# Rank counts as one column instead of 128, one comparison for five one-hots, and stores ahead of loads in an attention and expert kernel

## The chip, the cores and the metric

The program runs on 1 core of one Trainium2 chip. Its metric is the time of one execution on the device in microseconds (us): the median of 3 runs of the kernel before is 224.98 us (224.42 to 225.13). TensorE is called PE here, VectorE DVE, ScalarE ACT, GpSimd POOL, SyncE SP. SP only issues DMAs in this program; PEld is the part of PE that loads weights.

## What is computed

For 8 batches of 576 tokens, attention runs over 8 heads of width 64 in chunks of 64 tokens. Its output x (576 x 512 per batch) goes through a gated expert: each batch picks its 128 tokens with the highest gate score, those rows go through two matrix products, and the result is added back to them.

```python
scores = scale * np.matmul(q_c, k_c.transpose(0, 1, 2, 4, 3))       # per chunk of 64
attn = np.exp(scores - max); attn = attn / (np.sum(attn, axis=-1, keepdims=True) + 1e-09)
out = np.matmul(attn, v_c)                                          # -> x[b, token, 512]
scores = np.einsum('bsd,d->bs', x, w_gate)
for b in range(B):
    top_idx = np.argpartition(-scores[b], capacity)[:capacity]      # 128 of 576
    ye = np.maximum(x[b, top_idx] @ w1, 0.0) @ w2                   # 512 -> 1024 -> 512
    g = 1.0 / (1.0 + np.exp(-scores[b, top_idx]))
    out[b, top_idx] = x[b, top_idx] + g[:, None] * ye
```

## The kernel before, in words

**Units and steps.** The 4608 tokens are cut into 36 units of 128. A main loop runs one step after another (line 537). In step t it makes the scores of unit t, the transposes of unit t-1 and the values of unit t-2, so each unit passes through three steps: s (scores in PSUM), m and d (maximum and difference, DVE), t (transposes in PSUM), e (exponential, ACT), o (values in PSUM), den, rc and x (the normalised output, DVE). The tile x is stored to `out` and multiplied by the gate vector (prod, on POOL, summed by ACT; for units 8, 17, 26 and 35 by one DVE instruction), which gives one column of scores, sc.

**Ranking.** Nine units hold two batches: an even one of 4.5 units and an odd one. For each batch the scores are laid along a row by PE transposes (to_row), and DVE compares each of five blocks of tokens with the tokens before it and in it: cmp is the table of 0 and 1, and the same instruction counts its ones into a column of acc. The rank of a token is its count in acc plus what the later blocks have over it; that second part is the column sum of later blocks' cmp, so it is a PE product with cmp as the weights. rank_sums (line 305) makes it, and it makes it 128 columns wide, with a ramp 0..127 in a first product (ones against ramp), so that in every column k stands k minus the sum. rank_hot (line 322) compares that with acc and gives a one-hot table hot (token against rank); the last block, over which nothing stands, gets its own instruction from io and acc. rank_idx multiplies hot by token numbers and score parts (rt): idx are the 128 tokens, sg their scores. POOL then gathers those rows from `out` (xe), PE transposes them (expert_in), and two batches together make one round of expert products.

**The expert products.** ffn is a list of matmuls that the loop takes from in portions (quotas): so many after the scores, so many after place a, and so many after place b of a step. Each weight is split into a high part (ACT copies it into w1h, w2h) and a rest (POOL subtracts: w1l, w2l); a product is three matmuls. From the start of the first round on (step 13), PE always has such work to fill with.

**What sets the order.** Every engine takes its instructions in the order in which the program text issues them (class InOrder, line 62). Three tables set where the rarer parts stand: PLANS (lines 50 to 54) gives step and place of each ranking part for the first pair of batches (FIRST) and for the three other pairs (OTHER, 9 steps further for each pair), DOTS the units summed by DVE, WPLAN (line 58) for each of eight weight pieces the step of its load, and the places of its high part and its rest. The places of a step are, in order: pre, s0, s1, s2, a, b, c, d.

**Memory.** Inputs of a unit (qkvt, 772 KB) rotate through 5 buffers: the load of unit t+2 is issued in step t and waits for the values of unit t-3. Weights pass through 4 staging buffers (wst). One PSUM bank r serves all ranking parts and the transposes of xe, so each of these waits until the one before it has been read. SP issues loads, stores and weight loads in one queue; in a step the load stands ahead of the store, and the weight load behind both (lines 540 to 543).

Of the kernel before, what the change touches and what calls it, by code (L numbers as in the profile page):

```python
# [9 lines left out]
BF16 = mybir.dt.bfloat16  # L10
F16 = mybir.dt.float16
I32 = mybir.dt.int32
AF = mybir.ActivationFunctionType
ALU = mybir.AluOpType
# [6 lines left out]
CH = 64  # L21
CAP = 128
P = 128

NU = B * S // P
# [8 lines left out]
NTC = 5  # L34
# [14 lines left out]

FIRST = dict(rowe=(7, "a"), row4=(7, "b"), esum=(8, "s0"), ehot=(8, "s2"), eidx=(8, "b"), rowo=(10, "a"), row8=(10, "a"),  # L50
             osum=(11, "s0"), ohot=(11, "s2"), oidx=(11, "s2"), exin=(11, "a"), oxin=(12, "d"), ffn=(12, "d"))
OTHER = dict(rowe=(8, "b"), row4=(9, "b"), esum=(10, "a"), ehot=(10, "a"), eidx=(10, "c"), rowo=(11, "a"), row8=(11, "c"),
             osum=(12, "b"), ohot=(12, "b"), oidx=(13, "a"), exin=(13, "c"), oxin=(14, "c"), ffn=(14, "c"))
PLANS = (FIRST, OTHER, OTHER, OTHER)

DOTS = (8, 17, 26, 35)

WPLAN = ((9, (10, "c"), (11, "s0")), (10, (11, "c"), (11, "d")), (11, (12, "b"), (12, "d")), (12, (13, "b"), (13, "d")),
         (13, (14, "b"), (15, "d")), (14, (15, "b"), (16, "d")), (15, (16, "b"), (17, "d")), (16, (17, "b"), (18, "d")))


class InOrder:
# [22 lines left out]
def attention_moe(ctx: ExitStack, tc: tile.TileContext, qkv, wrep, w1, w2, consts, outs):  # L85
    nc = tc.nc
    pe, dve, act, pool, sp = (InOrder(tc, e) for e in (nc.tensor, nc.vector, nc.scalar, nc.gpsimd, nc.sync))

    cp = ctx.enter_context(tc.tile_pool(name="cp", bufs=1))
# [8 lines left out]
    con = cp.tile([P, C_N], F32, name="con")  # L98
    wr = cp.tile([P, DM], F32, name="wr")
    ltm = cp.tile([P, 5 * P], BF16, name="ltm")  # L100
    io = cp.tile([P, CAP], F16, name="io0")
    ones = cp.tile([33, P], BF16, name="ones")
    ramps = [cp.tile([33, 4, CAP], BF16, name=f"ramp{s}") for s in range(2)]
    accs = [cp.tile([P, NTC + 1], F32, name=f"acc{i}") for i in range(4)]
    one = cp.tile([P, CAP], BF16, name="one")
    ident = con[:, C_ID:C_ID + P]

    w1h = [cp.tile([P, NKT, 2 * P], F32R, name=f"w1h{k}") for k in range(NFT // 2)]
# [6 lines left out]
    def load(u, parts=None):  # L115
        t = iop.tile([P, UW], F32, name="qkvt")
        for e, lo, hi in parts or ((sp, 0, UW),):
            e.dma_start(out=t[:, lo:hi], in_=qkv[u][:, lo:hi])
        loaded[u] = t
# [23 lines left out]
    def scores(u):  # L143
# [4 lines left out]
        for h in range(HP):  # L148
            for r in range(2):
                R = slice(r * D, (r + 1) * D)  # L150
                for c in range(2):
                    pe.matmul(s[c * CH:(c + 1) * CH, r, h * CH:(h + 1) * CH], q[R, h, c, :], k[R, h, c, :],
                              start=True, stop=True)
# [16 lines left out]
    def r_bank(g, held=False):  # L170
        if g == 0 and not held:
            return ps_f.tile([P, 512], F32, name="f", tag="f")
        return ps_r.tile([P, 512], F32, name="r")
# [16 lines left out]
    def values(u):  # L190
        e = st_e.pop(u)
        v = loaded.pop(u)[:, 2 * QW:UW].rearrange("p (c h e) -> p c h e", c=2, h=HP)
        o = ps_v.tile([P, 2, 512], F32, name="o")
        for h in range(HP):
            for j in range(2):
                R = slice(j * CH, (j + 1) * CH)
                for c in range(2):
                    C = slice(c * CH, (c + 1) * CH)
                    pe.matmul(o[C, j, h * VW:(h + 1) * VW], e[R, h, C], v[R, c, h, :], start=True, stop=True)
        o4 = o[:, :, 0:HP * VW].rearrange("p j (h e) -> p j h e", e=VW)  # L200
        den = wk.tile([P, 2, HP], F32, name="den")
        act.activation(out=den, in_=o4[:, :, :, D], func=AF.Copy, bias=1e-9)
        st_o[u] = o4, den
# [45 lines left out]
    whole = slice(0, P)  # L249

    def blocks(s):


        if s == 0:
            return [(c, whole, c * P) for c in range(4)] + [(4, halves[0], 4 * P)]
        return [(4, halves[1], S)] + [(c, whole, c * P) for c in range(5, UPG)]
# [8 lines left out]
    def rank_cmp(b, i, row, part="all"):  # L265
# [4 lines left out]
        s = b % 2  # L270
        col, R, t0 = blocks(s)[i]
        n = R.stop - R.start
        before = t0 - s * S
# [30 lines left out]

    def rank_sums(b):


        r = rk[b]
        s = b % 2
        bl = blocks(s)  # L310
        cs = r_bank(b // 2, held=b == 0).rearrange("p (c k) -> p c k", c=4)
        for i in range(NTC - 1):
            Ri = bl[i][1]
            o = bl[i][2] - s * S
            n = Ri.stop - Ri.start
            pe.matmul(cs[Ri, i, :], ones[:, 0:n], ramps[s][:, i, :], start=True, stop=False)
            for j in range(i + 1, NTC):
                Rj = bl[j][1]
                pe.matmul(cs[Ri, i, :], r["cmp"][j][Rj, o:o + n], one[Rj], start=False, stop=(j == NTC - 1))
        r["cs"] = cs  # L320

    def rank_hot(b):
        r = rk[b]
        bl = blocks(b % 2)
        hot = r["hot"] = wk.tile([P, NTC, CAP], BF16, name="hot", bufs=2)
        for R, lo, hi in ((whole, 0, 4),) if b % 2 == 0 else ((bl[0][1], 0, 1), (whole, 1, 4)):
            n = hi - lo
            dve.tensor_tensor(
                out=hot[R, lo:hi, :], in0=r["cs"][R, lo:hi, :],
                in1=r["acc"][R, lo:hi].rearrange("p (c o) -> p c o", o=1).broadcast_to([R.stop - R.start, n, CAP]),  # L330
                op=ALU.is_equal)
        R = bl[4][1]
        dve.tensor_scalar(out=hot[R, 4, :], in0=io[R], scalar1=r["acc"][R, 5:6], scalar2=r["acc"][R, 4:5],
                          op0=ALU.subtract, op1=ALU.is_equal)

    rts = [cp.tile([P, NTC, 6], BF16, name=f"rt{i}") for i in range(4)]

# [123 lines left out]
    nload = 1  # L461
    while nload < NIO:
        load(nload)
        if nload == 2:
            sp.dma_start(out=wr, in_=wrep)
        nload += 1
    dve.memset(one, 1.0)
    dve.memset(ltm[:, 0:4 * P], -TINY)
    di = wk.tile([P, DF], F32, name="wst", bufs=4)
    pool.iota(di[:, 0:P], pattern=[[1, P]], base=0, channel_multiplier=-1, allow_small_or_imprecise_dtypes=True)  # L470
    dve.tensor_scalar(out=ltm[:, 4 * P:], in0=di[:, 0:P], scalar1=0.0, scalar2=-TINY, op0=ALU.is_lt, op1=ALU.mult)
    dj = wk.tile([P, DF], F32, name="wst", bufs=4)
    pool.iota(dj[:, 0:CAP], pattern=[[1, CAP]], base=0, channel_multiplier=0, allow_small_or_imprecise_dtypes=True)
    dve.tensor_copy(io, dj[:, 0:CAP])

    pool.iota(dj[0:1, 4 * CAP:8 * CAP], pattern=[[P, 4], [0, CAP]], base=-(4 * P), channel_multiplier=0,
              allow_small_or_imprecise_dtypes=True)
    dve.memset(ones, 1.0)
    for s, ramp in enumerate(ramps):
        dve.memset(ramp, 0.0)  # L480
        for c in range(4):
            dve.tensor_copy(ramp[32:33, c, :], dj[32:33, 0:CAP])
        dve.tensor_scalar(out=ramp[0:1].rearrange("p c k -> p (c k)"), in0=dj[0:1, 4 * CAP:8 * CAP],
                          scalar1=0.0 if s else float(CH), scalar2=None, op0=ALU.add)
    for i, rt in enumerate(rts):
        dve.tensor_copy(rt[:, :, 0:3], con[:, C_TOK + (i % 2) * 3 * NTC:C_TOK + (i % 2 + 1) * 3 * NTC]
                        .rearrange("p (c k) -> p c k", k=3))
# [5 lines left out]
    def at(when, f, *a, dt=0):  # L493
        events.setdefault((when[0] + dt, when[1]), []).append((f, a))

    fill = []
    for u in range(NU):
        c = u % UPG
# [6 lines left out]
    for g in range(NG):  # L505
        q = PLANS[g]
        t = UPG * g
        e, o = 2 * g, 2 * g + 1
        for f, k, a in (
# [5 lines left out]
            at(q[k], f, *a, dt=t)  # L515
    for i, (t, h, l) in enumerate(WPLAN):
        src, hi, lo = (w1, w1h, w1l) if i < 4 else (w2, w2h, w2l)
        at((t, "pre"), weight_load, src, i % 4)
        for k in range(2):
            at(h, weight_hi, src, i % 4, k, hi)  # L520
            at(l, weight_lo, src, i % 4, k, hi, lo)
# [9 lines left out]
    def run(step, place):  # L531
        for f, a in events.pop((step, place), []):
            f(*a)

    step = 0
    started = False
    while step < NU + 2 or events or fill:
        here = step < NU
        quota = [q for t, q in QUOTAS if t <= step][-1]
        if 2 < step and nload < NU:  # L540
            load(nload)
            nload += 1
        run(step, "pre")
        late = bool(fill)
        if late and 0 <= step - 2 < NU:
            values(step - 2)
        if here:
            scores(step)
        if not late:
            if 0 <= step - 1 < NU:  # L550
                transposes(step - 1)
            run(step, "s0")
            if 0 <= step - 2 < NU:
                values(step - 2)
        run(step, "s1")
        if late and 0 <= step - 2 < NU:
            normalise(step - 2)
        if here:
            maxima(step)
        run(step, "s2")  # L560
        if here:
            differences(step)
        if not late and 0 <= step - 2 < NU:
            normalise(step - 2)
        started = started or bool(fill)
        if not started:
            keep_warm(WARMS[min(step, len(WARMS) - 1)])
        run_fill(quota[0])
        if late and 0 <= step - 1 < NU:
            transposes(step - 1)  # L570
        run(step, "a")
        run_fill(quota[1])
        run(step, "b")
        run_fill(quota[2])
        run(step, "c")
        run(step, "d")
        step += 1


# [36 lines left out]
```

## Time and profile before

| what | value |
|---|---|
| median of 3 runs | 224.98 us (224.42 to 225.13) |
| profiled execution, its own time | 223.23 us |
| span of that profile | 221.5 us |
| mean granted TensorE clock | 0.955 |
| PE busy | 200.1 us (90% of the span), 3303 instructions |
| DVE busy | 134.3 us (61%), 345 instructions |
| POOL busy | 101.1 us (46%) |
| ACT busy | 79.0 us (36%) |
| DMA moved | 47.12 MB, mean 213 GB/s |

All terms are read in one profiled execution, whose own time, 223.23 us, is 1.73 us more than its span. The engines run side by side, so an engine's busy time says little by itself: what counts is, stretch by stretch, which engine or transfer the others wait for. A number in brackets at the end of a row of the timeline is the idle time of that engine in front of the row, and what ended it. Every row carries line 72, that of the helper that issues all instructions, so instructions are told apart by their tiles, written as out<-in.

### The profile page before, as it was taken

The numbers are of one execution on the slowest core, as the hardware profiler recorded it, in microseconds if no ns is written. First come the engines' busy times: TensorE is split into PE (matmuls) and PEld (weight loads), VectorE is DVE, ScalarE is ACT, GpSimd is POOL, SyncE is SP. The second block draws the span as 40 slices with busy tenths as digits, with TensorE's granted clock in tenths as the row PEclk, the third lists the DMA queues.
The fourth block names the chain that finished last, engine by engine and source line by source line (L and its number), as shares of the span: only waits on it lengthen the run. The fifth ranks groups of instructions, "written<-read, shape, count | busy, mean of one in ns | idle before, by whom it ended". The sixth has DMA issues, their size and how long they took to land.

```text
span 221.5 us, 7738 instructions
## 1 busy us (share of the span) xinstructions
PE 200.1 (90%) x3303; PEld 162.2 (73%) x3303; DVE 134.3 (61%) x345; ACT 79.0 (36%) x198; POOL 101.1 (46%) x116
## 2 busy tenths in 40 slices
PE   7787669699699989979999999899999989999990
PEld 2455547476599887667789988578899867899890
DVE  6578668767454377778685986666767644322120
ACT  2135322514448675112454553223455230212100
POOL 2024433356864699954464454508154671110031
PEclk9999996955799999999999999999999999999997
DMA  6999985998999887467899885658431110210011
GB/s 209 405 301 305 382 302 167 326 407 279 319 339 371 289 313 263 137 230 246 268 304 272 257 289 170 230 172 281 143 114 70 60 47 7 90 47 0 3 53 41
DMA packets 13777, 47.12 MB, mean 213 GB/s; under 512 B 1712, under 2 KB 2352, under 8 KB 13744
## 3 DMA queue, kind: packets, MB, share of 16 engines
q1 hardware_dynamic: 12160, 42.18, 55.7%
q0 software_dynamic: 1296, 4.20, 5.5%
q8 instruction: 26, 0.43, 0.8%
q10 hardware_dynamic: 288, 0.26, 0.4%
q14 instruction: 7, 0.06, 0.1%
HBM read 35.09 MB, written 11.53 MB: 211 GB/s over the span
## 4 chain that ended last, share of the span: by engine, by line
PE 49%; DVE 9%; POOL 7%; DMA 4%; ACT 4%; issue 2%; POOLq 1%; DVEq 0%
PE f L72 31%; PE r L72 7%; PE o L72 5%; PE s L72 3%; PE t L72 3%; DVE cmp L72 3%; DMA xe<-out,idx 3%; POOL prod L72 2%; POOL w2l L72 2%; POOL hl L72 2%; ACT prod L72 1%; DVE x L72 1%; DVE d L72 1%; DVE hot L72 1%; POOL w1l L72 1%
## 5 line engine op out<-in xcount | busy, mean ns | idle before, releaser
L72 POOL TENSOR_TENSOR prod<-x,wr 128x512 f32<-128x512 f32 x32 | 40.9, 1281 | 22.3 <-DVE x L72 22.1
L72 ACT ACTIVATE e<-t 128x512 f32<-128x512 f32 x36 | 21.5, 597 | 50.5 <-PE t L72 50.4
L72 PE MATMUL f<-xh,w1h 128*128 128x256 f32 x128 | 38.1, 297 | 0.0
L72 PE MATMUL f<-xl,w1h 128*128 128x256 f32 x128 | 36.8, 288 | 0.2 <-DVE ge L72 0.2
L72 PE MATMUL f<-xh,w1l 128*128 128x256 f32 x128 | 36.6, 286 | 0.0
L72 PE MATMUL o<-qkvt,e 64*64 64x65 f32 x1152 | 27.8, 232 | 4.0 <-issue 4.0
L72 PEld LDWEIGHTS o<-qkvt,e 64*64 64x64 f32 x1152 | 21.9, 141 | 9.8 <-issue 7.2
L72 PE MATMUL s<-qkvt 64*64 64x64 f32 x1152 | 26.4, 234 | 2.6 <-DMA qkvt<-qkv 2.1
L72 DVE TENSOR_TENSOR x<-o,rc 128x512 f32<-128x512 f32 x36 | 24.9, 692 | 6.2 <-DVE rc L72 2.8
L72 PE MATMUL f<-w2h,hh 128*128 128x512 f32 (+1 forms) x72 | 28.1, 391 | 0.0
L72 PEld LDWEIGHTS s<-qkvt 64*64 64x64 f32 x1152 | 22.5, 146 | 7.4 <-issue 2.1
L72 POOL DMA_INDIRECT out<-y,idx x9 | 9.1, 1006 | 39.7 <-DVE y L72 39.4
L72 PE MATMUL f<-w2l,hh 128*128 128x512 f32 (+1 forms) x72 | 27.1, 376 | 0.0
L72 PE MATMUL f<-w2h,hl 128*128 128x512 f32 (+1 forms) x72 | 27.0, 375 | 0.0
L72 DVE TENSOR_REDUCE m<-s 128x8 f32<-128x512 f32 x36 | 24.6, 683 | 3.8 <-PE s L72 3.7
L72 DVE TENSOR_TENSOR d<-s,m 128x512 f32<-128x512 f32 x36 | 24.9, 691 | 1.2
L72 POOL TENSOR_TENSOR hl<-hr,hh 128x512 fp32r<-128x512 f32 x12 | 15.4, 1286 | 20.9 <-ACT hh L72 16.9
L72 PEld LDWEIGHTS f<-xh,w1h 128*128 128x128 f32 x128 | 24.3, 190 | 0.9
L72 PEld LDWEIGHTS f<-xl,w1h 128*128 128x128 f32 x128 | 24.4, 190 | 0.8 <-DVE ge L72 0.4
L72 ACT ACTIVATE prod<-prod 128x512 f32<-128x512 f32 x32 | 20.0, 626 | 12.4 <-POOL prod L72 12.4
L72 PEld LDWEIGHTS f<-xh,w1l 128*128 128x128 f32 x128 | 24.3, 190 | 0.2
L72 PE MATMUL t<-con,d 128*128 128x128 f32 x144 | 23.4, 287 | 0.0
(74 smaller groups left out, 283.3 us busy)
## 6 DMA issues: line engine op xcount, KB each, us to landing
qkvt<-qkv SPq DMA_DIRECT2D x35, 772.0 KB, 5.6
out<-x SPq DMA_DIRECT2D x32, 256.0 KB, 4.9
wst<-w SPq DMA_DIRECT2D x8, 512.0 KB, 6.6
out<-x SPq DMA_DIRECT2D x8, 128.0 KB, 3.9
qkvt<-qkv SPq DMA_DIRECT2D x1, 260.0 KB
qkvt<-qkv ACTq DMA_DIRECT2D x2, 128.0 KB, 3.1
qkvt<-qkv SPq DMA_DIRECT2D x2, 128.0 KB, 2.9
wr<-wrep SPq DMA_DIRECT2D x1, 256.0 KB, 6.8
```

The costliest lines, as they stand in the source:

```text
L72: ins = f(*a, **k).ins
```

## The change

1. **Sums.** rank_sums now makes one column per block instead of 128. Two products with the identity (ident, in con) copy acc's columns into PSUM, one of five columns and one for the second count of the last block; ten products of a cmp block with a column of minus ones follow in the same bank. ones, ramps and one are gone.
2. **One-hots.** rank_hot is one comparison of 640 columns, of a table io5 (two versions, made at the start) with the five sums, each spread over 128 columns. It was two instructions for even batches and three for odd ones. All four acc tiles are set to zero at the start.
3. **Places.** For pairs 2 to 4: the last block's row and comparison (row8) go from place c of step 11 to place a of step 12; the odd sums and one-hots (osum, ohot) from b to c of step 12; the odd index and gather (oidx) from a to b of step 13.
4. **SP.** Place pre, with the store, now runs before the load of the step; in step 11 the load goes to the end of the step.
5. **Weights.** The first w1 piece is loaded in step 11 instead of 9, the second at the end of 11 instead of in 10, the third at the end of 12 instead of in 11. Their high parts go to 12 a, 12 d and 13 b (from 10 c, 11 c, 12 b), their rests to 12 b, 13 s1 and 13 d (from 11 s0, 11 d, 12 d). The five pieces behind them are loaded, copied and split exactly one step later.

```diff
-OTHER = dict(... row8=(11, "c"), osum=(12, "b"), ohot=(12, "b"), oidx=(13, "a"), ...)
+OTHER = dict(... row8=(12, "a"), osum=(12, "c"), ohot=(12, "c"), oidx=(13, "b"), ...)
-WPLAN = ((9, (10, "c"), (11, "s0")), ...
+WPLAN = (((11, "s1"), (12, "a"), (12, "b")), ...
...
-        cs = r_bank(b // 2, held=b == 0).rearrange("p (c k) -> p c k", c=4)
+        cs = r["cs"] = r_bank(b // 2, held=b == 0)[:, 0:NTC]
+        pe.matmul(cs, ident, r["acc"][:, 0:NTC], start=True, stop=False)
+        pe.matmul(cs[:, 4:5], ident, r["acc"][:, 5:6], start=False, stop=False)
...
-            pe.matmul(cs[Ri, i, :], ones[:, 0:n], ramps[s][:, i, :], start=True, stop=False)
             for j in range(i + 1, NTC):
                 Rj = bl[j][1]
-                pe.matmul(cs[Ri, i, :], r["cmp"][j][Rj, o:o + n], one[Rj], start=False, stop=(j == NTC - 1))
+                pe.matmul(cs[Ri, i:i + 1], r["cmp"][j][Rj, o:o + n], minus[Rj], start=False, stop=(i, j) == (NTC - 2, NTC - 1))
...
-        for R, lo, hi in ((whole, 0, 4),) if b % 2 == 0 else ((bl[0][1], 0, 1), (whole, 1, 4)):
-            n = hi - lo
-            dve.tensor_tensor(
-                out=hot[R, lo:hi, :], in0=r["cs"][R, lo:hi, :],
-                in1=r["acc"][R, lo:hi].rearrange("p (c o) -> p c o", o=1).broadcast_to([R.stop - R.start, n, CAP]),
-                op=ALU.is_equal)
-        R = bl[4][1]
-        dve.tensor_scalar(out=hot[R, 4, :], in0=io[R], scalar1=r["acc"][R, 5:6], scalar2=r["acc"][R, 4:5],
-                          op0=ALU.subtract, op1=ALU.is_equal)
+        dve.tensor_tensor(out=hot, in0=io5[b % 2], in1=r["cs"].rearrange("p (c o) -> p c o", o=1).broadcast_to([P, NTC, CAP]),
+                          op=ALU.is_equal)
...
-        at((t, "pre"), weight_load, src, i % 4)
+        at(t, weight_load, src, i % 4)
...
-        if 2 < step and nload < NU:
+        run(step, "pre")
+        if 2 < step and step != 11 and nload < NU:
             load(nload)
             nload += 1
-        run(step, "pre")
...
         run(step, "d")
+        if step == 11:
+            load(nload)
+            nload += 1
         step += 1
```

**Place one: the odd sums of the second pair (step 21), on PE.** Names: sc are score columns, o and s values and scores of two units, t transposes, f expert products, cmp the comparison tables. Before:

```order
L72 MATMUL r<-con,sc 128x128
L72 MATMUL o<-qkvt,e 64x65 x16
L72 MATMUL s<-qkvt 64x64 x16
...
L72 MATMUL t<-con,d 128x128 x4
L72 MATMUL f<-w2h_99,hh_1162 128x512
L72 MATMUL f<-w2l_103,hh_1162 128x512
L72 MATMUL f<-w2h_99,hl_1163 128x512
L72 LDWEIGHTS ones
L72 MATMUL r<-ramp_85,ones 64x128
L72 LDWEIGHTS cmp_1703
L72 MATMUL r<-one,cmp_1703 64x128
```

The same place with the change:

```order
L73 MATMUL o<-qkvt,e 64x65 x16
L73 MATMUL s<-qkvt 64x64 x16
...
L73 MATMUL t<-con,d 128x128 x4
L73 MATMUL r<-con,sc 128x128
L73 MATMUL f<-w2h_97,hh_1140 128x512
...
L73 MATMUL f<-w2h_98,hl_1237 128x512
L73 MATMUL r<-acc_87,con 128x5
L73 MATMUL r<-acc_87,con 128x1
L73 LDWEIGHTS cmp_1684
L73 MATMUL r<-minus,cmp_1684 64x1
```

The last block's transpose (r<-con,sc) has gone from the end of a step to the middle of the next one, and the sums behind three more expert products. Each sum used to have 14 pairs of weights and matmul (4 with ones, 10 with cmp); now it has the two identity products and 10 pairs.

**Place two: the same stretch on DVE.** m and d belong to step 21, y is the end of an expert round. Before:

```order
L72 SCALAR_TENSOR_TENSOR cmp_1709,acc_89<-r,sc,ltm 128x448
L72 SCALAR_TENSOR_TENSOR cmp_1709,acc_89<-r,sc,ltm 128x128
...
L72 TENSOR_TENSOR d<-s,m 128x2x4x64
L72 SCALAR_TENSOR_TENSOR y<-f,g,xe 128x512
L72 TENSOR_TENSOR hot<-r,acc_89 64x128
L72 TENSOR_TENSOR hot<-r,acc_89 128x384
L72 TENSOR_SCALAR hot<-io_82,acc_89 128x128
```

With the change:

```order
L73 SCALAR_TENSOR_TENSOR cmp_1690,acc_87<-r,sc,ltm 128x448
...
L73 TENSOR_TENSOR d<-s,m 128x2x4x64
L73 SCALAR_TENSOR_TENSOR y<-f,g,xe 128x512
L73 SCALAR_TENSOR_TENSOR cmp_1690,acc_87<-r,sc,ltm 128x128
L73 TENSOR_TENSOR hot<-io_83,r 128x640
```

The last comparison stood ahead of the step's rc, x, m and d; it now stands behind them and behind y, right in front of the one-hot.

**Place three: SP, steps 9 to 13.** qkvt is the load of a unit, out its store, wst a weight piece. Before:

```order
L72 DMA qkvt<-qkv 128x1544
L72 DMA out<-x 128x512
L72 DMA wst<-w 128x1024
L72 DMA qkvt<-qkv 128x1544
L72 DMA out<-x 128x512
L72 DMA wst<-w 128x1024
```

With the change, from the store of step 11 on:

```order
L73 DMA out<-x 128x512
L73 DMA wst<-w 128x1024 x2
L73 DMA qkvt<-qkv 128x1544
L73 DMA out<-x 128x512
L73 DMA qkvt<-qkv 128x1544
L73 DMA wst<-w 128x1024
L73 DMA out<-x 128x512
L73 DMA wst<-w 128x1024
L73 DMA qkvt<-qkv 128x1544
```

The three DMAs of a step before went load, store, weight; now the store, which waits for x, stands in front, and the first weight pieces come two steps later in a bunch.

## Rows read from the trace of the kernel before

**Rows 1.** Windows: busy us (instructions) per engine, granted clock, DMA share, GB/s.
```profile
5.00:36.00 31.00, 24.28 (x588) 16.69 (x590) 21.83 (x52) 9.78 (x27) 8.39 (x10) 0.97 0.87 314
36.00:60.00 24.00, 20.32 (x376) 14.43 (x376) 15.63 (x43) 9.81 (x26) 15.10 (x16) 0.71 0.94 324
60.00:90.00 30.00, 28.96 (x551) 25.63 (x544) 18.42 (x43) 18.23 (x43) 22.48 (x22) 0.98 0.91 322
90.00:191.50 101.50, 98.02 (x1622) 81.28 (x1621) 68.38 (x181) 36.64 (x95) 50.08 (x59) 1.00 0.55 179
```

**Rows 2.** Timeline of PE from 90 us: start us, length us, instruction, [idle before <-releaser].
```profile
91.64 0.18 PE L72 MATMUL r<-rt,hot 64*128 64x6 bf16 x1 [0.47 <-DVE hot L72]
...
97.30 0.29 PE L72 MATMUL r<-con,sc 128*128 128x128 f32 x1 [1.21 <-DVE cmp L72]
...
139.65 0.29 PE L72 MATMUL r<-con,sc 128*128 128x128 f32 x1 [0.90 <-DVE cmp L72]
...
179.88 0.29 PE L72 MATMUL r<-con,sc 128*128 128x128 f32 x1 [0.64 <-DVE cmp L72]
```

**Rows 3.** Chain that ended last: start us, us on the chain, what.
```profile
100.71 1.64 PE r L72 x14
...
105.09 0.44 PE t L72 x4
105.53 0.29 PE r L72 x5
...
130.63 1.52 PE r L72 x14
...
133.88 0.20 PE r L72 x5
```

**Rows 4.** Timeline of PE in step 11: first instruction of the sums, first behind them.
```profile
46.40 0.31 PE L72 MATMUL f<-ramp,ones 33*64 33x128 bf16 x1
...
48.84 1.15 PE L72 MATMUL o<-qkvt,e 64*64 64x65 f32 x32
```

**Rows 5.** Tile hot: count, ns min/median/max, first and last start, forms.
```profile
L72 DVE TENSOR_TENSOR hot<-r,acc x10: 295/558/692, 34.2 to 184.0; 128x512 bf16<-128x512 f32 x4, 64x128 bf16<-64x128 f32 x3, 128x384 bf16<-128x384 f32 x3
```

**Rows 6.** Timeline of DVE, steps 19 and 21.
```profile
90.16 0.69 DVE L72 TENSOR_TENSOR hot<-r,acc 128x512 bf16<-128x512 f32 x1
90.77 0.81 DVE L72 TENSOR_SCALAR hot<-io,acc 64x128 bf16<-64x128 f16 x1
...
100.21 0.69 DVE L72 TENSOR_TENSOR d<-s,m 128x512 f32<-128x512 f32 x1
100.81 0.74 DVE L72 SCALAR_TENSOR_TENSOR y<-f,g,xe 128x512 f32<-128x512 f32 x1
```

**Rows 7.** Timeline of POOL, 90 to 151 us.
```profile
90.25 1.28 POOL L72 TENSOR_TENSOR prod<-x,wr 128x512 f32<-128x512 f32 x1
91.49 2.53 POOL L72 TENSOR_TENSOR w2l<-wst,w2h 128x512 fp32r<-128x512 f32 x2
...
106.93 1.00 POOL L72 DMA_INDIRECT xe<-out,idx  x1 [2.73 <-DVE sg L72]
...
150.68 1.01 POOL L72 DMA_INDIRECT out<-y,idx  x1 [0.30 <-issue]
```

**Rows 8.** Timeline of PE: transposes of gathered rows in steps 12 and 23.
```profile
57.58 0.75 PE L72 MATMUL r<-con,xe 128*128 128x128 f32 x4 [1.67 <-DMA xe<-out,idx]
...
110.80 0.63 PE L72 MATMUL r<-con,xe 128*128 128x128 f32 x4
```

**Rows 9.** Tile xe: its gathers from issue to landing.
```profile
DMA to landing us min/median/max: 3.3/4.0/6.7
```

**Rows 10.** Timeline of SP, steps 4 and 5: load of unit 6, store of unit 1.
```profile
15.93 0.33 SPq L72 DMA_DIRECT2D qkvt<-qkv  x1
17.17 0.34 SPq L72 DMA_DIRECT2D out<-x  x1
```

**Rows 11.** Timeline of PE: scores of unit 6.
```profile
22.35 0.69 PE L72 MATMUL s<-qkvt 64*64 64x64 f32 x32 [1.10 <-DMA qkvt<-qkv]
```

More of the change, by code (lines that the diff above doesn't have):

```diff
@@ L51 @@
              osum=(11, "s0"), ohot=(11, "s2"), oidx=(11, "s2"), exin=(11, "a"), oxin=(12, "d"), ffn=(12, "d"))
-OTHER = dict(rowe=(8, "b"), row4=(9, "b"), esum=(10, "a"), ehot=(10, "a"), eidx=(10, "c"), rowo=(11, "a"), row8=(11, "c"),
-             osum=(12, "b"), ohot=(12, "b"), oidx=(13, "a"), exin=(13, "c"), oxin=(14, "c"), ffn=(14, "c"))
+OTHER = dict(rowe=(8, "b"), row4=(9, "b"), esum=(10, "a"), ehot=(10, "a"), eidx=(10, "c"), rowo=(11, "a"), row8=(12, "a"),
+             osum=(12, "c"), ohot=(12, "c"), oidx=(13, "b"), exin=(13, "c"), oxin=(14, "c"), ffn=(14, "c"))
 PLANS = (FIRST, OTHER, OTHER, OTHER)
 DOTS = (8, 17, 26, 35)
-WPLAN = ((9, (10, "c"), (11, "s0")), (10, (11, "c"), (11, "d")), (11, (12, "b"), (12, "d")), (12, (13, "b"), (13, "d")),
-         (13, (14, "b"), (15, "d")), (14, (15, "b"), (16, "d")), (15, (16, "b"), (17, "d")), (16, (17, "b"), (18, "d")))
+WPLAN = (((11, "s1"), (12, "a"), (12, "b")), ((11, "d"), (12, "d"), (13, "s1")), ((12, "d"), (13, "b"), (13, "d")),
+         ((13, "pre"), (14, "b"), (14, "d")), ((14, "pre"), (15, "b"), (16, "d")), ((15, "pre"), (16, "b"), (17, "d")),
+         ((16, "pre"), (17, "b"), (18, "d")), ((17, "pre"), (18, "b"), (19, "d")))
 class InOrder:
@@ L100, in attention_moe @@
     ltm = cp.tile([P, 5 * P], BF16, name="ltm")
-    io = cp.tile([P, CAP], F16, name="io0")
-    ones = cp.tile([33, P], BF16, name="ones")
-    ramps = [cp.tile([33, 4, CAP], BF16, name=f"ramp{s}") for s in range(2)]
+    io5 = [cp.tile([P, NTC, CAP], F16, name=f"io5{s}") for s in range(2)]
     accs = [cp.tile([P, NTC + 1], F32, name=f"acc{i}") for i in range(4)]
-    one = cp.tile([P, CAP], BF16, name="one")
+    minus = cp.tile([P, 1], BF16, name="minus")
     ident = con[:, C_ID:C_ID + P]
@@ L315, in rank_sums @@
             n = Ri.stop - Ri.start
-            pe.matmul(cs[Ri, i, :], ones[:, 0:n], ramps[s][:, i, :], start=True, stop=False)
             for j in range(i + 1, NTC):
                 Rj = bl[j][1]
-                pe.matmul(cs[Ri, i, :], r["cmp"][j][Rj, o:o + n], one[Rj], start=False, stop=(j == NTC - 1))
-        r["cs"] = cs
+                pe.matmul(cs[Ri, i:i + 1], r["cmp"][j][Rj, o:o + n], minus[Rj], start=False, stop=(i, j) == (NTC - 2, NTC - 1))
     def rank_hot(b):
         r = rk[b]
-        bl = blocks(b % 2)
         hot = r["hot"] = wk.tile([P, NTC, CAP], BF16, name="hot", bufs=2)
-        for R, lo, hi in ((whole, 0, 4),) if b % 2 == 0 else ((bl[0][1], 0, 1), (whole, 1, 4)):
-            n = hi - lo
-            dve.tensor_tensor(
-                out=hot[R, lo:hi, :], in0=r["cs"][R, lo:hi, :],
-                in1=r["acc"][R, lo:hi].rearrange("p (c o) -> p c o", o=1).broadcast_to([R.stop - R.start, n, CAP]),
-                op=ALU.is_equal)
-        R = bl[4][1]
-        dve.tensor_scalar(out=hot[R, 4, :], in0=io[R], scalar1=r["acc"][R, 5:6], scalar2=r["acc"][R, 4:5],
-                          op0=ALU.subtract, op1=ALU.is_equal)
+        dve.tensor_tensor(out=hot, in0=io5[b % 2], in1=r["cs"].rearrange("p (c o) -> p c o", o=1).broadcast_to([P, NTC, CAP]),
+                          op=ALU.is_equal)
     rts = [cp.tile([P, NTC, 6], BF16, name=f"rt{i}") for i in range(4)]
@@ L466, in attention_moe @@
         nload += 1
-    dve.memset(one, 1.0)
+    dve.memset(minus, -1.0)
     dve.memset(ltm[:, 0:4 * P], -TINY)
@@ L472, in attention_moe @@
     dj = wk.tile([P, DF], F32, name="wst", bufs=4)
-    pool.iota(dj[:, 0:CAP], pattern=[[1, CAP]], base=0, channel_multiplier=0, allow_small_or_imprecise_dtypes=True)
-    dve.tensor_copy(io, dj[:, 0:CAP])
-    pool.iota(dj[0:1, 4 * CAP:8 * CAP], pattern=[[P, 4], [0, CAP]], base=-(4 * P), channel_multiplier=0,
+    pool.iota(dj[:, 0:NTC * CAP], pattern=[[P, NTC], [1, CAP]], base=-(4 * P), channel_multiplier=0,
               allow_small_or_imprecise_dtypes=True)
[L478 to L484, printed above, removed]
+    for s in range(2):
+        for lo, hi in ((0, 4), (4, 5)):
+            dve.tensor_scalar(out=io5[s][:, lo:hi].rearrange("p c k -> p (c k)"), in0=dj[:, lo * CAP:hi * CAP],
+                              scalar1=float(CH) if s == 0 and lo == 0 else 0.0, scalar2=None, op0=ALU.add)
+    for acc in accs:
+        dve.memset(acc, 0.0)
     for i, rt in enumerate(rts):
```

## The prediction

> **What bounds the kernel now.** I read the windows first. They cut the span into four regimes [rows 1]. From 5 to 36 us the DMA engines are the busiest thing (share 0.87) and PE is busy 24.28 of 31.00 us. From 36 to 60 us the granted clock averages 0.71, so PE spends much of it at the lower of its two levels (1.2 of 2.4 GHz), and the DMA share is 0.94. From 60 to 90 us PE is busy 28.96 of 30.00 us with the DMA still at 0.91 and POOL at 22.48. From 90 us to 191.5 us PE is busy 98.02 of 101.50 us at full clock and the DMA has room (0.55). So after 90 us every microsecond taken from PE's list, and every one in which PE stands, counts nearly once; before 60 us it is transfers, waits and the clock.
>
> Then the timeline of PE, for rows with idle time in front. Past 90 us the larger ones all stand in the ranking [rows 2]: three times PE waits in front of the last block's transpose because DVE still reads the bank with the other blocks (1.21, 0.90 and 0.64 us), once for the second half of a one-hot (0.47). Last, the chain, for what ranking itself costs there: a batch's sums are 14 matmuls in 1.52 us (the rows with 1.64 take in 0.12 of the neighbour), the five index products 0.20 to 0.29, four 128-column transposes 0.44 [rows 3].
>
> **Sums.** Before, 14 pairs of 128-column weights and 128-column matmul cost 1.52 us, 109 ns a pair. After, ten pairs have one column. The nearest row is the index product, five pairs with the same weights and six columns in 0.20 to 0.29: 40 to 58 ns each, so ten take 0.40 to 0.58. The two identity products are fp32. An fp32 product shows in this trace as two passes per matmul (the 16 scores matmuls of a step are 32 instructions [rows 11]), so they are four passes; no row has 128 x 128 fp32 weights with few columns. A pass costs no less than an index pair (40 ns) and no more than a transpose (0.44/4 = 110 ns): 0.16 to 0.44. Together 0.56 to 1.02; I take 0.85, near the upper end because fp32 passes are nearer to the transposes. A batch saves 1.52 - 0.85 = 0.67. Six batches (2 to 7) lie past 80 us on a busy PE: **-4.0 us** (from -3.0 to -5.8).
>
> Batches 0 and 1 lie in front. For batch 0 the sums cannot be finished before DVE's last comparison, old or new: 0. Batch 1 stands at the slow clock, and its sums take 48.84 - 46.40 = 2.44 us of a PE that does not stop [rows 4]; at the same ratio 1.36 remain: **-1.1** (0 to -1.5).
>
> Beside the numbers of this trace stands a rule of the Trainium skill ("TensorE: Matmul & The Clock Gate", section "LDWEIGHTS (loading the stationary operand)"): loading weights takes their columns divided by 1.2 GHz, however few columns follow, which is 107 ns for 128. The index products, 40 to 58 ns for load and matmul, do not agree with it. By that rule fourteen loads would be worth 1.5 us and the saving zero; it is a rival below.
>
> **The waits of rows 2.** The transpose of the last block moves behind the next step's transposes; the bank it needs has been read by then. The 0.47 goes because the one-hot is one instruction. Gone: 1.21 + 0.90 + 0.64 + 0.47 = 3.22, **-3.2**.
>
> **One-hots on DVE.** From 128 x 128 to 128 x 512 the old comparison grows from 295 to 692 ns, 1.03 ns a column [rows 5], so 640 columns take 0.82 (bounds 0.69, the 512-column row, and 1.0, two old instructions). Before it was 0.69 and more: in step 19 the second part took 0.81 for 64 x 128, ending at 91.58 when POOL's prod ended at 91.53 [rows 6, 7], while the first part, with an input in PSUM, ran beside the same prod at its usual 0.69. The new one also has its second input in PSUM, so I let it run freely. The Trainium skill ("SBUF — State Buffer", section "two separate sides") calls the port pair of VectorE and GpSimd an exclusive lock, taken by two-port modes or two SBUF inputs; these rows agree with it. Without it the new comparison could be stretched as well, worth up to 0.7 us in a step where PE waits for it.
>
> **New waits.** Step 19: DVE is at the one-hot from 90.16, so it is ready at 90.98 instead of 91.58. That is 0.6 better, but PE would come 0.67 earlier and already lost 0.47: of the 1.14 counted above 0.54 is not had, +0.5. Step 21: the last comparison (0.4, from the 0.30 of a 128-column instruction [rows 5] and the write of its count) now stands behind d and y, which end at 101.55 [rows 6]; it ends at 101.95 in the old frame, and PE, which reached its sums at 100.71 [rows 3], now has three products (0.7) more in front, so it waits 0.5 to 0.6 (0 to 1.2). Step 39: no attention work is left between the two requests for the bank, so about half of the 0.64 comes back, +0.3. Odd gathers: index products move one third of a step back. The second pair's gather was issued at 106.93; a landing takes 3.3 to 4.0 [rows 7, 9], so 110.23 to 110.93, and PE used it at 110.80 [rows 8]: no slack. DVE's queue held that index up before, so I charge only 0.2. For the third pair the scatter of y (150.68, 1.01 of POOL) now stands in front of the gather: 0.4. For the last pair 0.2. The rests of w2 come a step later, and the last (2.53 of POOL, [rows 7]) behind a gather of 1.00: 0.5. Sum 0.5 + 0.6 + 0.3 + 0.8 + 0.5 = **+2.7**. Each of these could vanish or double: +0.5 to +5.5.
>
> **Stores ahead of loads.** The load of unit 6 was issued at 15.93, the store now ahead of it at 17.17 [rows 10], so the load comes 17.17 + 0.34 - 15.93 = 1.6 later, and so for every load. Units 5 to 7 had no slack: PE already waits 1.10 for unit 6 [rows 11]. But the DMA engines are nearly full there, so what a load loses the store gains; a late issue costs only what the queue runs dry. I take **+0.7**, with bounds of -0.3 (stores and weights out of the way) and +3 (units 5, 6 and 7 each in full, partly shared). From unit 8 on, loads are issued three steps ahead and absorb 1.6.
>
> In return the store that batch 1's gather needs leaves earlier, the two w1 pieces that shared the DMA before it are gone, and its index is 1.1 earlier. PE waited 1.67 for that gather [rows 8]: **-1.0** (0 to -1.7). The weights needed from step 13 on arrive one step ahead instead of two; splitting them is POOL work of equal size.
>
> The setup (less DVE work, one wider iota) lies under the first loads: 0, either way at most 0.5.
>
> **The sum.** -4.0 - 1.1 - 3.2 + 2.7 + 0.7 - 1.0 = -5.9. Against the profiled execution's own time, 223.23 - 5.9 = 217.3. That execution lies 1.75 under the median of the runs, 224.98, so for a median I say 224.98 - 5.9 = **219.1 us**.
>
> **Rivals.**
> *Weights decide (7%).* If a one-column pair costs as much as a 128-column one, the -4.0 and -1.1 vanish: 224.2. For it: before, load and matmul took 109 ns together. Against it: the index products.
> *Late feeders (17%).* The six places above cost 1 us each because a gather, a scatter or a w2 rest blocks PE's list: +6 instead of +2.7, 222.4. For it: the gather without slack and POOL at 75% between 60 and 90 us. Against it: PE's own list is shorter by less than the feeders' chains.
> *Starved loads (9%), the slower side.* A load waits for x, x waits for values, values wait for the load of five units before; if the queue runs dry, 1.6 is lost in each of the rounds at units 5, 8, 11 and 14: +6.4 instead of +0.7, and the gather's 1.0 is not gained. PE stands more, and the clock of 36 to 60 us (0.71, so 7 us lost in 24) stays as low for 12 more: +3.5. Sum -5.9 + 5.7 + 1.0 + 3.5 = +4.3, 229.3. It decides when the loads cost over 6.6 in all. For it: 1.10 at unit 6. Against it: a DMA share near 0.9 leaves little to run dry.
> *Clock (11%).* The waits at 41 to 58 us that keep PE slow get shorter, and half of the 7 us comes back: -9.5, 215.5.
>
> **How the numbers follow.** The forecast has 56% and its own range 216.5 to 221.5. For 8 in 10 I add the clock case and most of the late feeders, and cut off half of the first rival and the slower side: 214.5 to 224.0. A difference under 0.3% (0.7 us) cannot be told from none. Faster: 56 + 11 + nearly all of 17 + a part of 7 = 0.85; same 0.06; slower 0.09.
>
> **What would show it.** Sums of batches 2 to 7: 12 short products in 0.85; near 1.5 the first rival holds, and the forecast falls by four. No idle row with "DVE cmp" in front of r<-con,sc in steps 20 and 29. In step 21 a wait of about 0.6 in front of the identity product. One-hot rows of 0.82, also beside prod. Scores of units 5 to 7 later by under 1 us in sum; later by 3 or growing at units 8 and 11, the loads starve. No wait for xe in step 12, or one under 0.7. Gathers of odd batches within 0.5 us of PE. A clock in 36 to 60 us far from 0.71 would move the whole by more than any of these.

## The result, and the profile after

The changed kernel takes **217.77 us** (median of 4 runs, 216.53 to 219.5) where the kernel before takes 224.7 (223.83 to 225.13): ratio 0.9702, 95% interval 0.9613 to 0.979. The forecast was 219.1. The profiled execution took 216.53 us (span 214.7), 6.70 less than that of before. The sum of -5.9 was nearly right; its split was not. Executions of one kernel differ by some per cent, so the ratios below leave out a kernel's slower ones, and the profiles of runs 6 and 7 are of slower executions.

Windows of the changed kernel (columns as in [rows 1]):

```profile
36.00:60.00 24.00, 21.08 (x446) 16.54 (x445) 17.48 (x44) 10.34 (x28) 11.94 (x14) 0.80 0.87 296
60.00:90.00 30.00, 26.61 (x554) 23.41 (x547) 17.83 (x44) 18.39 (x45) 28.07 (x26) 1.00 0.92 347
```

Between 36 and 60 us the granted clock averages 0.80 instead of 0.71. Between 60 and 90 us POOL's busy time has gone from 22.48 to 28.07 of 30 us, and PE, no longer packed, from 28.96 to 26.61. Timeline of PE, the rows with idle time in front that answer to [rows 2, 8]:

```profile
53.99 0.60 PE L73 MATMUL r<-con,xe 128*128 128x128 f32 x4
...
64.83 0.27 PE L73 MATMUL o<-qkvt,e 64*64 64x65 f32 x2 [1.06 <-issue]
71.40 0.55 PE L73 MATMUL t<-con,d 128*128 128x128 f32 x3 [0.89 <-issue]
...
87.81 0.50 PE L73 MATMUL f<-w2l,hh 128*128 128x512 f32 x1 [1.33 <-POOL w2l L73]
92.81 0.50 PE L73 MATMUL f<-w2l,hh 128*128 128x512 f32 x1 [0.21 <-POOL w2l L73]
...
97.83 0.61 PE L73 MATMUL r<-acc,con 128*128 128x5 f32 x4 [0.36 <-DVE cmp L73]
107.29 0.63 PE L73 MATMUL r<-con,xe 128*128 128x128 f32 x4 [0.61 <-DMA xe<-out,idx]
...
149.99 0.63 PE L73 MATMUL r<-con,xe 128*128 128x128 f32 x4 [1.09 <-DMA xe<-out,idx]
```

The first row has no wait: batch 1's gather is in time in this profile. All four waits of [rows 2] are gone, and five others, of 3.60 together, stand in their place (2.78 in run 9, the same kernel again). The chain has the sums of four batches, answering to [rows 3], and tile hot the one-hot, answering to [rows 5]:

```profile
97.83 1.06 PE r L73 x14
...
127.47 1.01 PE r L73 x14
...
139.15 0.79 PE r L73 x14
...
168.07 1.00 PE r L73 x14
```

```profile
L73 DVE TENSOR_TENSOR hot<-io,r x7: 809/822/822, 34.2 to 177.9; 128x640 bf16<-128x640 f16 x7
```

An even batch's sums (x14) now cost 1.00 on the chain and an odd one's 0.79, or 1.06 where they stand behind a wait (batch 3, first row); the one-hot takes 0.82 wherever it stands.

To see where the 6.7 us come from I cut each span at two places that every trace shows: the first scores matmul of step 14 (expert products begin in step 13) and that of step 35 (at 163.45 before and 158.97 in the changed kernel). What lies behind the second is called the tail. The first scores of step 14, before and changed:

```profile
63.98 0.65 PE L72 MATMUL s<-qkvt 64*64 64x64 f32 x32
...
59.75 0.64 PE L73 MATMUL s<-qkvt 64*64 64x64 f32 x32
```

The table gives us against the profile of the kernel before, one profile each; before has 63.98, 99.47 and 57.99 in its three parts.

| kernel | to step 14 | 14 to 35 | tail | sum |
|---|---|---|---|---|
| changed | -4.23 | -0.24 | -2.24 | -6.71 |
| sums and one-hots alone | +0.02 | -2.45 | -1.38 | -3.82 |
| order and weights alone | -3.16 | +2.26 | -0.02 | -0.92 |
| changed, old places | -3.71 | -1.07 | -1.38 | -6.16 |
| changed, again | -2.84 | -1.37 | -2.23 | -6.44 |

The tail repeats to 0.04 us: the nine profiles that share the changed kernel's tail, or move only an index product in it, have 55.77 to 55.81. The first two parts move by more than 1 us between the two profiles of one kernel (first and last row). Up to step 14 the program text of runs 3, 4, 7, 8, 9, 10 and 11 is that of the changed kernel, and in seven of these eight profiles the first part lies from -4.23 to -1.61, in run 7's at +0.32. Among what differs are the stretches at half clock, loads, and the stalls of the last section. So a single profile carries a cause there only where it shows the wait itself, and a difference under 2.6 us in the first part is no difference.

### The profile page after: what moved, and what is told of

Its sections match the earlier page's. It is cut to its first block, busy times and chain, and to the rows that moved or that the text cites. A ratio compares the mean times of both kernels' runs of the same rounds, so it can differ in the third digit from the quotient of the medians.

```text
span 214.7 us, 7721 instructions
## 1 busy us (share of the span) xinstructions
PE 191.9 (89%) x3298; PEld 161.2 (75%) x3303; DVE 129.0 (60%) x327; ACT 78.8 (37%) x198; POOL 101.1 (47%) x115
## 4 chain that ended last, share of the span: by engine, by line
PE 56%; DMA 6%; DVE 3%; POOL 3%; issue 2%; ACT 1%; POOLq 1%; DVEq 0%
PE f L73 37%; PE o L73 7%; PE r L73 5%; PE s L73 4%; DMA xe<-out,idx 4%; PE t L73 4%; DVE x L73 2%; POOL w2l L73 1%; DMA out<-y,idx 1%; DMA out<-x 1%; POOL hl L73 1%; POOL prod L73 1%; DVE m L73 1%; POOLq L602 1%; DVE y L73 1%
## 5 line engine op out<-in xcount | busy, mean ns | idle before, releaser
L73 PE MATMUL o<-qkvt,e 64*64 64x65 f32 x1152 | 26.7, 229 | 2.4 <-issue 1.8
L73 PEld LDWEIGHTS o<-qkvt,e 64*64 64x64 f32 x1152 | 21.3, 138 | 7.6 <-issue 5.0
L73 PE MATMUL t<-con,d 128*128 128x128 f32 x144 | 23.9, 290 | 0.9 <-issue 0.9
```

Of the source, the lines that this page charges most:

```text
L73: ins = f(*a, **k).ins
```

## Experiments

Runs 1 to 4, 5 to 8 and 9 to 12 each shared one chip and the runs of the kernel before on it (medians 225.38, 226.47 and 225.18 us). The brackets behind a ratio are its 95% interval.

**1. Sums and one-hots alone.** The kernel before with the new rank_sums, rank_hot and their tables.


> The kernel before with the new sums and one-hots alone (places, weight plan and order of stores and loads as before). My theory: batches 2 to 7 save 0.6 to 0.7 us each past 80 us, batch 1 saves 1 to 1.5, the 0.47 us wait for the second half of a one-hot goes; the three waits in front of the last block's transpose stay. -4.5 to -6 us against the kernel before. Rival (order): what the changed kernel gains by step 14 (4.2 us) is mostly due to the order of stores, loads and weights, through the gather of batch 1 and the clock; then this run gains only the later sums, -3 to -4.


Measured: 219.93 us, ratio 0.9774 (0.9708 to 0.9839), -5.1 by the ratio: within my theory, though the interval (-3.6 to -6.6) holds a part of the rival too. Its profile (-3.8) lies with the rival and shows what neither said. At the start of step 12 it leads by 3.74 (48.65 against 52.39), then PE stands for batch 1's gather and all of it is gone. Timeline of POOL and PE:

```profile
49.62 1.01 POOL L72 DMA_INDIRECT xe<-out,idx  x1 [3.87 <-DMA out<-x]
...
56.70 1.09 PE L72 MATMUL r<-con,xe 128*128 128x128 f32 x4 [5.09 <-DMA xe<-out,idx]
```

The gather is issued 1.94 us earlier than before (49.62 against 51.56), but lands only 6.9 us after its issue, where before it took 5.9.

**2. Order and weights alone.** The kernel before with the new WPLAN and loop.


> The kernel before with the new order of stores and loads and the later weights alone (old sums, one-hots and places). My theory: loads +0.7, gather of batch 1 -1.0, rests of w2 +0.5: -1 to +1.5 us against the kernel before. Rival (order): it carries the early gain, -2.5 to -4. Rival (starved loads): +2 or more.


Measured: 222.52, ratio 0.9894 (0.9827 to 0.9962), -2.4 (-0.9 to -3.9): beyond my theory, and nearly what the rival said. By step 14 its profile leads by 3.16, as the rival wants: its gather, issued at 51.30, lets PE start at 55.00, where it waits only for DVE; before, issued at 51.56, PE started at 57.58. Then 2.26 are given back, 1.37 of it to the load of unit 15, which now stands behind a store and a bunch of weights:

```profile
66.49 0.69 PE L73 MATMUL s<-qkvt 64*64 64x64 f32 x32 [1.37 <-DMA qkvt<-qkv]
```

**3. Old places.**
```diff
-row8=(12, "a"), osum=(12, "c"), ohot=(12, "c"), oidx=(13, "b")
+row8=(11, "c"), osum=(12, "b"), ohot=(12, "b"), oidx=(13, "a")
```


> The changed kernel with the old places of the last transpose, odd sums, one-hots and index products. My theory: the waits in front of the last transpose (1.21 + 0.90 + 0.64 before) come back, the waits for xe (0.61 + 1.09) and for the last comparison (0.36) that the changed kernel shows go: +0.5 to +1.2 us against the changed kernel, about 218.7. Rival (feeders): the places cost as much as they bring or more: 0 to -1.


Measured: 218.58, ratio 0.9739 (0.9676 to 0.9801): no difference from the changed kernel that can be told. Beside run 2, which differs from it by the sums and one-hots alone, it is 0.0155 lower in ratio, 3.5 us, with intervals that do not meet. The waits for the last comparison are back, and those for xe in batches 3 and 5 are gone, as said; between steps 14 and 35 the two about cancel. In the tail, which repeats, the places are worth 2.24 - 1.38 = 0.86, and the sums and one-hots 1.36 (57.99 in run 2, 56.63 here).

**4. Index products earlier,** `oidx=(13, "a")` in the changed kernel; and **10, the same again** beside **9, the changed kernel again.**


> The changed kernel with the odd index products one place earlier (in front of the second share of FFN work). My theory: the gathers of batches 3 and 5 are issued 0.7 and over 1.3 us earlier, the third pair's in front of the scatter of y; PE's two waits for xe (0.61 and 1.09) go: -1.2 to -1.7 us against the changed kernel, about 216.3. Rival (POOL): the scatter or prod that now comes behind the gather blocks PE or the next store's reader, 0 to -0.5.

> The changed kernel itself, so that the three runs beside it have it on the same chip. Expected: 0.970 of the kernel before (0.963 to 0.977), with a wait for w2l of about 1.3 us in steps 19 to 20 and waits for xe in batches 3 and 5.

> The early index products once more, beside the changed kernel. Theory: the waits for xe in batches 3 and 5 (0.61 + 1.09) go again and the time is 0.5 to 1.7 us less. Rival: the 1.9 us between the first two runs came from the spread between chips; then within 0.5 us.


Measured: ratios 0.9617 (0.9551 to 0.9684), then 0.9739 (0.9631 to 0.9847) for the changed kernel and 0.9782 (0.9695 to 0.9868) for this. Against the changed kernel's first ratio it looked like 1.9 us; beside the changed kernel on one chip it is nothing that can be told, as the last rival said. The waits for xe do shrink (from 0.64 and 0.77 to 0.60 and 0.43 in the second pair of profiles, to none in the first), but the parts from 14 to 35 agree within 0.1 us (98.10 for the changed kernel again, 98.15 and 98.14 for these). The changed kernel's first profile has 99.23 there, so up to 1 us stays open.

**5. Loads in front of stores again,** the weights late as changed.
```diff
+        if 2 < step and step != 11 and nload < NU: load(...)
         run(step, "pre")
-        if 2 < step and step != 11 and nload < NU: load(...)
```


> The changed kernel with each step's load in front of its store again (weights later, as changed). Theory (stores open the gather): the half batch that the gather of batch 1 needs leaves behind a load of 772 KB, the gather lands 1 to 2 us later, and of the 4.2 us gained by step 14 one to three go: +1 to +3 us against the changed kernel, although the scores of unit 6 come 1 us earlier. Rival (weights open it): it is the weight loads that left the queue free; then 0 to -1 (the loads' 1 us comes back).


Measured: 219.69, ratio 0.9752 (0.9673 to 0.9832), not told apart from the changed kernel. Its gather, issued at 50.55, has PE start at 56.16, behind x; run 8, whose code up to step 17 is that of the changed kernel, starts at 56.72 on the same chip. Step 14 starts at 61.35, among the 59.75 to 62.37 of the runs with stores first. So the order of stores and loads is not what brings step 14 forward.

**6. Old plan of the weights,** stores first as changed.


> The changed kernel with the old plan of the weights (stores in front of loads, as changed). Theory (stores open the gather): the gather still lands in time, the waits for w2l (1.33 + 0.21) and part of those between 60 and 75 us go: -1 to -2 us against the changed kernel. Rival (weights open it): two 512 KB loads stand in front of the gather of batch 1 again, it lands at 56 us or later and PE waits 2 to 5 us: +1 to +4.


Measured: 217.39 once, the five others 222.91 to 224.66, median 223.13 against 226.47. With one execution so far from the others the time decides nothing. The profile, of 222.95 us, lies with the rival: PE waits longer for this gather than in any other run:

```profile
60.50 1.08 PE L72 MATMUL r<-con,xe 128*128 128x128 f32 x4 [5.49 <-DMA xe<-out,idx]
```

Run 8 started it 3.8 earlier. That is one pair; all the profiles together say this. With the early pieces (before, runs 1 and 6) step 14 starts at 63.98, 64.00 and 66.93, and batch 1's gather lands 5.9 to 7.0 us after its issue. With the late ones step 14 starts at 59.75 to 62.37 in ten profiles and at 64.30 in run 7's, and the gather takes 3.5 to 6.8. With loads first in both cases, before and run 1 stand against run 5 (61.35). So the late pieces bring step 14 forward, by some 2.6 us there. That they do it through the gather alone is not shown, since the landings overlap: with one and the same text up to step 14, PE waits for this gather nothing in three profiles and 0.30, 1.11, 1.39, 2.01 and 3.03 in five.

**7. Two half rests of w2 on DVE,** with the index products early.
```diff
-        pool.tensor_tensor(out=half(lo[i], k), ...
+        e = dve if hi is w2h and i > 1 and k == 0 else pool
+        e.tensor_tensor(out=half(lo[i], k), ...
```


> The changed kernel with the index products one place earlier (as in the run of that name) and the first half of the last two rests of w2 on DVE in place of POOL. Theory: DVE takes 0.7 us for what takes POOL 1.3; POOL reaches the rests that PE waits for (1.33 + 0.21) early enough: -1 to -1.5 us against the run with the early index products alone. Rival (DVE): in steps 18 and 19 DVE's list carries comparisons for the next pair, and x or d come 0.7 later each: 0 to +1.


Measured: 222.34, ratio 0.9801 (0.9714 to 0.9888), slower than with the early index alone in run 4 (0.9617) but not told apart from it in run 10 (0.9782), both on other chips. The gain of the theory is not there. The profile, of 223.21 us, shows a wait that stands against it (how much of its 101.34 from step 14 to 35, against 98.15 and 98.14 with the early index alone, is that execution's own stays open). The rest stood ahead of x in DVE's queue and took 1.73 beside POOL (0.68 when alone, at 93.55); DVE's prod behind it, at 90.48 beside a rest on POOL, took 1.73 as well, and the one-hot came late:

```profile
86.58 1.73 DVE L73 TENSOR_TENSOR w2l<-wst,w2h 128x512 fp32r<-128x512 f32 x1
...
93.01 0.36 PE L73 MATMUL r<-rt,hot 128*128 128x6 bf16 x5 [2.24 <-DVE hot L73]
...
93.55 0.68 DVE L73 TENSOR_TENSOR w2l<-wst,w2h 128x512 fp32r<-128x512 f32 x1
```

**8. Ten pairs twice.** In rank_sums of batches 2 to 7 the ten products stand once more in front, into columns that nobody reads.


> The changed kernel with the ten one-column products of batches 2 to 7 issued twice (the first time into columns that nobody reads). They measure about 0.45 us (odd batch) and 0.6 us (even) in the trace. Theory (PE's list sets the time past 80 us): all of it is paid, 3 x 0.45 + 3 x 0.6 = +3 us against the changed kernel, less 0.5 for waits that shrink: +2.3 to +3.2. Rival (waits decide there): PE waits for w2l, xe and the last comparison anyway, +1 or less.


Measured: 222.2, ratio 0.9844 (0.9761 to 0.9927), +2.4 to +3.2 against the two ratios of the changed kernel, as the theory has it, but with intervals that overlap. The tail, which repeats, is the sharper test. The chain:

```profile
172.38 1.85 PE r L73 x24
...
182.19 1.35 PE r L73 x24
```

So ten more pairs cost 0.85 (even) and 0.56 (odd), 1.41 for the two batches of the tail, and the tail is 57.10 instead of 55.77: 1.33 of the 1.41 is paid. There the theory holds and the rival does not.

**11. Rests of w2 one step earlier** (places d of steps 15 to 18 instead of 16 to 19), with the index early.


> Early index products, and the four rests of w2 one step earlier, as they were in the kernel before (their loads and first halves stay late). Theory: step 15 has no rest, so POOL has room there; the wait for w2l (1.3 to 1.6) goes: -1 to -1.6 us against the run with early index products alone. Rival (POOL is full between 60 and 90 us): hl or the gather of batch 2 come later by what w2l gains, 0 to +1.


Measured: 216.99, ratio 0.9693 (0.962 to 0.9766). The wait for w2l is gone from the trace; it was 1.20 and 0.26 in run 10, and the ratios differ by 2.0 us, with intervals that overlap. The profile does not show the gain: PE now waits 1.66 for batch 3's gather (0.60 in run 10), and the part from 14 to 35 takes 98.74 instead of 98.14.

**12. PE kept busy in two idle places,** added to run 11.
```diff
+    for when, f0, n in (((8, "s0"), rank_sums, 3), ((10, "a"), compare_last, 3)):
+        at0 = [f for f, _ in events[when]].index(f0)
+        events[when].insert(at0, (keep_warm, (n,)))
```


> The kernel with the early rests, and three more junk matmuls in each of two idle places of PE: before batch 0's sums (idle 1.43 us) and before the transpose for the last block of pair 1 (idle 0.7 to 0.9 us). Theory (idle PE brings the half clock): one or two of the three stretches at half clock between 23 and 53 us go, -0.5 to -2 us against the run with early rests. Rival (the transfers set the pace there): the time stays within 0.5 us, though the clock is higher.


Measured: 215.89, ratio 0.9669 (0.9596 to 0.9742). The stretches at half clock that run 11 has at 37 to 40 and 47 to 54 us are gone; the window reads 0.93 where run 11 has 0.79. At the start of step 12 it leads run 11 by 3.1, and then:

```profile
36.00:60.00 24.00, 17.28 (x388) 13.61 (x392) 17.17 (x46) 8.71 (x25) 13.13 (x15) 0.93 0.90 329
```

```profile
55.45 0.63 PE L73 MATMUL r<-con,xe 128*128 128x128 f32 x4 [4.33 <-DMA xe<-out,idx]
```

Up to step 14 the rival holds: a faster PE waits for the gather, falls to half clock behind that wait (56 to 59 us), and step 14 starts at 61.88, not before run 11's 61.41. This has the lowest median of all, but its interval does not part it from the changed kernel's, and what its profile leads by comes between steps 14 and 35, where both programs are the same (96.47 against 98.74).

## Why the prediction was right in sum and wrong in its split

**Sums of batches 2 to 7 (-4.0): right.** Taken 0.85 each, measured 1.00 and 0.79 on the chain. Alone, they and the one-hots bring 2.45 + 1.38 = 3.83 past step 14, and 0.69 a batch in the tail, where 0.67 was forecast for the sums. They are the part that the times show too: -5.1 alone, and 3.5 between runs 2 and 3. Run 8 shows that PE pays in the tail for every pair. The reading by the index product was too good (40 to 58 ns a pair; run 8 has 85 in an even batch, with 128 columns, and 56 in an odd one, where some have 64); the margin taken for fp32 made up for it. The Trainium skill ("TensorE: Matmul & The Clock Gate", section "LDWEIGHTS (loading the stationary operand)") has 107 ns for 128 columns: the pairs of run 8 lie below that, and the saving is there, so "weights decide" falls.

**Stores ahead of loads and the gather of batch 1 (+0.7 - 1.0): the step that failed.** Forecast at -0.3 together, the order and the weights measure -2.4 by the time of run 2 (-0.9 to -3.9); in its profile -3.2 at step 14, of which 2.3 is lost again up to step 35. I had bounded the gather by the wait that PE showed, 1.67. But its landing is what step 13 starts from: a PE that comes earlier waits longer (5.09 in run 1, 4.33 in run 12), and a landing that comes earlier lets the whole list move. Runs 5 and 6 say that the late weights do it, not the stores that I had argued from; "the two w1 pieces that shared the DMA before it are gone" stood in half a sentence. How much of it goes through the gather stays open (run 6).

**Batch 1's sums (-1.1): not seen in the time.** The sums themselves go from 2.44 to 0.95 us of PE (46.70 to 47.65, behind a wait of 0.58 for the last comparison), at full clock where before they stood at half. But alone they bring nothing at step 14 (run 1, +0.02). Under the new order run 3 starts step 14 0.55 earlier than run 2 and the changed kernel 1.07, both less than profiles of the same text differ.

**Clock: no term of the sum, and the rival did not come.** The window rose from 0.71 to 0.80, so (0.80 - 0.71) x 24 = 2.2 of the 7 us came back, less than the rival's half. The seven other profiles with the same text up to step 14 read 0.74 to 0.86 and run 1, with the old order, 0.78, so even this can't be put down to the change. In run 12, at 0.93, what the clock gave was waited away by step 14.

**Waits gone (-3.2) and new waits (+2.7).** All four went. The new ones are 1.33 + 0.21 for w2l (forecast 0.5), 0.36 for the last comparison (0.5 to 0.6), 0.61 and 1.09 for xe (0.2 and 0.4): 3.60 in this profile, 2.78 in run 9's. The 0.5 of step 19 is covered by w2l; where that wait goes, it appears (0.18 in run 11, 0.83 in run 12). The 0.3 for the bank and the 0.2 for the last gather were not due: the tail gains 0.86 by the places, not 0.64 - 0.5. The step missed is POOL: its late rests crowd the stretch in which it also makes hl and prod. The two halves of the rest that PE waits 1.33 for:

```profile
86.01 2.99 POOL L73 TENSOR_TENSOR w2l<-wst,w2h 128x512 fp32r<-128x512 f32 x2
```

Its first half took 1.75 us beside DVE's prod of unit 17 (0.68, from 85.96), where the other halves take 1.27 to 1.29; so up to 0.47 of the 1.33 is that. The rival "late feeders" had the place right; of its 3.3 above the forecast 0.9 came, or 0.1 by run 9. And a wait taken away is not a gain yet: run 11 has none for w2l, and its part from 14 to 35 is no shorter.

**Starved loads.** Here step 6 starts 1.12 later (PE waits 2.56 for unit 6 instead of 1.10) and step 8 no later than before, as forecast. But in the ten other profiles with stores first PE waits 2.1 to 3.6 for unit 6 (0.08 and 0.26 in runs 1 and 5, with loads first), and step 8 starts 0.5 to 2.6 later than before: about the upper half of the +0.7's bounds. Not all of that is the order, since run 5 has step 8 1.13 later too, behind an "issue" stall of 1.87. Later loads starve where I held them safe: unit 15 in runs 2 and 9 (1.37 and 1.16).

What stays open: how much of the part from 14 to 35 is lost to which wait, since it moves by 1.1 us between two profiles of one kernel; and whether order, weights and places together bring anything beyond the sums, since run 1 (0.9774) and the changed kernel (0.9702 and 0.9739) have intervals that overlap.

## What to carry to other kernels

Where a transfer's landing starts the next stretch, price a change by that landing (issue plus time under way), not by the wait in front of it: the wait is only what the other side has left over, and a gain on one side alone can be swallowed by the other (run 1 led by 3.74 at step 12 and by nothing at step 14). Before a stretch of one profile is put down to a change, see how far it moves between profiles of the same text. And look for a part of the span that repeats to a few hundredths (here the tail) to price small terms; a ratio with an interval of a per cent either way can't.

## What was not expected of the hardware

In every trace here PE has stalls that the profile calls "issue", idle time in which it waits for nothing shown, of 0.2 to 1.9 us inside a group of matmuls, mostly o or t and mostly before 85 us, that end 1.2 to 1.6 us after a 16 KB packet of the instruction queue has been moved: in the changed kernel packets end at 14.03, 63.44 and 70.11 and PE goes on at 15.33, 64.83 and 71.40; before, at 40.31 and 80.10, and 41.58 and 81.41. Of the 26 packets of a run, 3 have such a stall behind them in the changed kernel and 5 before. The page of the profile has this queue in one row:

```profile
q8 instruction: 26, 0.43, 0.8%
```

The Trainium skill ("Runtime: NRT & Kernel Launch", section "Instruction fetch mechanics") says that the sequencer fetches blocks of 16 KB by its own DMA queue and that this is mostly hidden. The size agrees. With the DMA share near 0.9 it is not always hidden: 1.06 + 0.89 = 1.95 us between 60 and 90 us of the changed kernel. No run here tests it by taking the other transfers away.
